# Attention rounds of 11, 10 and 11 key tiles in place of rounds of 8, and the output weights made in the last stage

## The chip, the cores and the metric

The kernel runs on one core of a Trainium2 chip. The metric is the device time of one execution in microseconds; lower is better. Every number below is from the hardware profiler's record of one execution, or from the times of unprofiled runs.

The core has a matmul engine (TensorE, PE in the profile, with its weight loads shown as PEld), three other compute engines (VectorE or DVE, ScalarE or ACT, GpSimd or POOL) and SyncE (SP), which here only starts transfers. Each works through its own queue in order. An instruction that needs another engine's result waits for a semaphore, and everything queued behind it on its engine waits with it. Matmul results go to PSUM, eight banks of 128 x 512 float32, and must be read from there by DVE or ACT before the bank can be used again.

## The reference

S = 2048 tokens, D = 448 features, H = 16 heads of 28 features, F = 1792 hidden features. What matters here:

```
g = sigmoid((x * gate_w).sum(-1, keepdims=True))
q, k, v = (x @ wqkv) per head
a = softmax(q k^T * 28 ** -0.5) @ v, heads joined, @ wo
gate = x @ W_gate;  up = x @ W_up
b = (relu(gate) * up) @ W_down
out = g * a + (1 - g) * b
```

## The kernel before, in words

Large matmuls run on float32r numbers; products of weights and tokens are made of a high and a low part of each, in 11 terms (`TERMS`, `NT = 11`) per output tile. The program has three stages.

**Projections.** q, k and v are made for all heads, and q and k go to memory. Between them stand the first matmuls of the softmax maxima.

**Attention rounds.** This is the long stage, and the change is in it. For a head, scores are computed as 16 key tiles of 128 keys by 2048 queries, and each key tile as 4 matmuls of 512 queries (`scores`, L202), which ACT turns into exp values in a buffer of 128 x 2048 (`P` slot, L204). The row maxima that the exp needs come from a separate pass over the transposed scores (`smax`, L175): 64 matmuls a head, each read by DVE with a maximum over 512 columns (L176). When a head's 64 are done, the maxima are transposed on PE (`smax_end`, L183) and sent by ACT, POOL and a transfer into two extra rows of `Q`, so that the scores come out with the maximum already subtracted. The maxima run 24 key tiles ahead of the scores. In the same stage PE makes the gated layer: a unit is 128 hidden features for 512 tokens, and has two halves, gate and up, of 11 matmuls each (`gu_mm`, L497). ACT applies relu to the gate half (`relu`), DVE multiplies it with the up half and POOL sends the product to memory (`spill_h`).

The order of these matmuls on PE is written out by hand as strings, one letter a matmul: `s` a score matmul, `m` a maximum matmul, `x` a matmul of the gated layer. `h` stands for the last of the 11 matmuls of two halves together: it needs only 64 of the array's 128 rows, so the two run side by side, each on its own rows (a pair). A round is one string followed by `pv`, which multiplies the exp values of all the round's key tiles with V (L531), four 32-column matmuls side by side, and adds into `OS` on DVE. There are `NP = 8` P slots, so a round has 8 key tiles and a head two rounds: 32 rounds, one with `FIRST`, 28 with `LONG` or `WIDE` (30 or 40 `x`, three or four halves), three with `LATE`.

Each kind of matmul has its own PSUM banks: `ps_s` gives the scores banks 0 and 1 in turn, `ps_m` gives the maxima banks 3 and 2 in turn, `ps_f` gives the halves 4, 5, 6, 7. At the start of a round `later` lends the scores and maxima a bank of a half that has not begun. In the `LATE` rounds, which have no maxima left, `ps_p` turns the scores through banks 0 to 3.

At a round's end ACT and POOL split the weights of the next units into high and low parts (`split_f`) and SP fetches the raw weights after them (`fetch_f`, two buffers). `small_things` starts the loads of K and Q two heads ahead, and handles the softmax denominators of the head before: the sums leave `OS` by a transfer (`ls`, L540), DVE takes reciprocals (`row_sums`, L545), they go out (`l_d`) and come back spread over the partitions (`spread`, `rb`, L552), and `normalise` multiplies `OS` with them and sends it out (`o_d`).

In the `LATE` rounds the output weights come back from memory (`load_wo`) and are split into high and low parts (`split_wo`); their tile `WO` is held in the attention stage's memory.

**Last stage.** The remaining units, the down projection (`down`, L751) and the output projection (`wout`, L706) alternate on PE by a list `todo`. SP fetches what they need (`fetch_d`: `wdr` and `hr`), and ACT, DVE and POOL split it (`split_d`).

Of the kernel before, what the change touches and what calls it, by code (L numbers as in the profile page):

```python
# [8 lines left out]
F32 = mybir.dt.float32  # L9
# [9 lines left out]
P = 128  # L19
S = 2048  # L20
# [21 lines left out]

FIRST = "ssssssssssssssssmmmmssulxxxsxxxsxmmsxsxxmmxsxsmmxxsxsmmxsxsxmmsxsxxmmssx"

LONG = "smsmxsmmsxxsmxsmxsmxsmxsmxsmxsmxsmxsmxsmxsmxsmxsmxsmxsmxsmxsmxsmxsmxsmxsmxsmxsmxsmxsmxsmxsmxsm"
WIDE = "smsmxsmmsxxsmxsmxsmxxsmxsmxsmxxsmxsmxsmxxsmxsmxsmxxsmxsmxxsmxsmxsmxxsmxsmxsmxxsmxsmxsmxxsmxsmxsmxxsmxsmxhh"
# [22 lines left out]
def gated_mix_kernel(ctx, tc, x, wq, wo, wgu, wd, out):  # L71
# [19 lines left out]
    def ps_s():  # L91
        return banks[turn("s", (0, 1))]
# [16 lines left out]
    def ps_f():  # L109
        return banks[turn("f", (4, 5, 6, 7))]  # L110

    def later(n):

        return banks[4 + (count["f"] + 1 + n) % 4]

    def act_high(dst, src):
        nc.scalar.activation(dst, src, AF.Copy)  # L117
# [76 lines left out]

    PT = {}

    def scores(i, j, ps=None):
        h, kt = divmod(i, NK)
        if j == 0:
            PT[i] = p_slot(i % NP, f"P_{i}")  # L200
        ps = ps or (ps_s() if i < NI - 3 * NK // 2 else ps_p())
        nc.tensor.matmul(ps, K[h % 3][:GD + 2, kt * P:(kt + 1) * P], Q[h][:GD + 2, j * TB:(j + 1) * TB],  # L202
                         start=True, stop=True)
        nc.scalar.activation(PT[i][:, j], ps, AF.Exp, scale=SCALE)  # L204
# [18 lines left out]
    with tc.tile_pool(name="qkv", bufs=1) as pa:  # L223
# [146 lines left out]
        x1 = load_x(1)  # L370


        warm = const.tile([P, TB], BF16, name="warm")
        nc.vector.memset(warm, 0.0)
        ps = ps_x()
        for n in range(WARM):
# [49 lines left out]
        for n, (f, *a) in enumerate(mixed):  # L426
            if n == 0:
                split_w(*w5)
            if n == 6:
                load_k(1)  # L430
                load_q(1)
            if n == 8:
                split_w(*w3)
            if n == 13:

                nc.gpsimd.memset(f32(K[2])[96:128], -1.0)
            if n == len(mixed) - 6:
# [8 lines left out]
            news = [(scores, *divmod(k, NB)) for k, back in enumerate(EARLY) if back == len(mixed) - n]  # L446
# [18 lines left out]
    att = stk.enter_context(tc.tile_pool(name="att", bufs=1))  # L465

    done = sum(n for _, n in ROUNDS) // 2
    SECOND = set(range(ROUNDS[0][1] + 1, 2 * done, 2))

    def lane(k):  # L470
        return slice(64 * k, 64 * k + 64)
# [19 lines left out]
    def gu_mm(ps, i, s, n):  # L491

        a, b = (BY_CHUNK if i else HIGH_FIRST)[n]
        rows = slice(0, P)
        if n == NT - 1 and 2 * i + s in SECOND | {k - 1 for k in SECOND}:
            rows = lane(int(2 * i + s in SECOND))
        nc.tensor.matmul(ps, WS[i][rows, s, a], xf(i // NF, b)[rows], start=(n == 0), stop=(n == NT - 1))  # L497
# [23 lines left out]

    OS, LS = {}, {}

    def pv(i0, ni):

        h = i0 // NK
        po = ps_w() if i0 == 0 else ps_m() if i0 < NI - 3 * NK // 2 else ps_p()
        for i in range(i0, i0 + ni):
            p = PT.pop(i)
            for j in range(NB):  # L530
                nc.tensor.matmul(po[32 * j:32 * j + 32], V[:, h // 4 % 2, i % NK, h % 4], p[:, j], start=(i == i0),  # L531
                                 stop=(i == i0 + ni - 1))
        if i0 % NK == 0:
            OS[h] = fe.tile([P, TB], F32, name=f"os_{h}", tag="os", bufs=2)
            nc.vector.tensor_copy(OS[h], po)  # L535
        else:
            nc.vector.tensor_tensor(OS[h], po, OS[h], op=OP.add)  # L537
        if (i0 + ni) % NK == 0:
            LS[h] = fe.tile([P, 16], F32, name=f"ls_{h}", tag="ls", bufs=2)
            nc.gpsimd.dma_start(LS[h], OS[h][DH::32].rearrange("j (p c) -> j p c", c=16))  # L540
# [26 lines left out]
    def load_wo():  # L567
        r = f32(q_slot("wor"))
        nc.sync.dma_start(r[:, 0:3, :D], wo_d[0:3 * P].rearrange("(c p) n -> p c n", p=P))
        for a in (0, 64):  # L570
            nc.sync.dma_start(r[a:a + 64, 3, :D], wo_d[3 * P:])
        return r[:, :, :D]

    def split_wo(r):
        dve_high(WO[:, 0:3], r[:, 0:3])
        pool_low(WO[:, 3:6], r[:, 0:3], WO[:, 0:3])
        dve_high(WO[:, 6], r[:, 3])
        pool_low(WO[64:, 6], r[64:, 3], WO[64:, 6])

    nxt = parts = i0 = 0  # L580

    def small_things(u):

        h, q = divmod(u, 4)

        if q == 0 and h and h + 2 < H:
            load_k(h + 2)
            load_q(h + 2)
        if u in (16, 32):
            g = u // 16 + 1  # L590
            nc.sync.dma_start(V[:, g % 2], v_d[g])
        if u == 2:
            pack_wo()
        if h and q == 2:
            row_sums(h - 1)
            spread(h - 1)

    split_f(0, act_high, pool_low, (0,))
    fetch_f(1)
    wor, units = None, []  # L600
    for r, (order, nu) in enumerate(ROUNDS):
        ni = order.count("s") // NB
        late = order == LATE
        todo = list(range(nxt, nxt + nu))
        nxt += nu
        small_things(i0 // 4)
        rest = []
        if m % (4 * NK) == 0 and i0 <= NI - LEAD:
            rest = smax_end(m // (4 * NK) - 1, later(2))
            rest.pop(0)()  # L610
            while late and rest:
                rest.pop(0)()
        if late and wor is None:
            wor = load_wo()

        passes = [(*divmod(k, 2), n) for k in todo for n in range(NT - (r > 0))]
        ns = 0
        for n, o in enumerate(order):
            if o == "s":
                i, j = i0 + ns // NB, ns % NB  # L620
                if ns == 4 * NB:
                    small_things(i0 // 4 + 1)
                if len(EARLY) <= i * NB + j:

                    scores(i, j, later(1) if r and ns == 2 and not late else None)
                ns += 1
                if rest and ns == 3:
                    rest.pop(0)()
            elif o == "m":

                smax(m, ps_w() if r == 0 else later(1) if order[:n].count("m") == 1 else ps_m())
                m += 1
            elif o == "x":
                i, half, k = passes.pop(0)
                if k == 0:
# [5 lines left out]
            elif o == "l":  # L641
                sends.pop()()
            elif o == "u":
                split_f(0, act_high, pool_low, (1,))
                load_k(2)
                load_q(2)
                fetch_f(2)
                parts = 2
            elif o == "h":
                ends, units = units[:2], units[2:]  # L650
                for i, half, ps in ends:
                    gu_mm(ps, i, half, NT - 1)
                for i, half, ps in ends:
                    spill_h(i, ps) if half else relu(i, ps, late)
        assert not passes, (r, passes)

        ready = nxt + (ROUNDS[r + 1][1] if r + 1 < len(ROUNDS) else 2)
        ready += ready % 2
# [6 lines left out]
        if i0 == NK // 2:  # L665
            gates()
        if i0 > NK and i0 % NK:
            normalise(i0 // NK - 1)
        pv(i0, ni)
        i0 += ni  # L670
        if late and i0 == NI - NK // 2:
            split_wo(wor)
    assert i0 == NI and m == 4 * NK * H and not units, (i0, m)
    stk.close()


    pf = ctx.enter_context(tc.tile_pool(name="ffn", bufs=1))
    ON, OR, GA, DR, HH, ACC = {}, {}, {}, {}, {}, {}

    def fetch_o(tb):  # L680
        OR[tb] = r = pf.tile([P, 4, TB], F32, name=f"or_{tb}", tag="or", bufs=1)
# [110 lines left out]
    for tb, load, split, at in ((0, 2, (3, 4), (5, 6, 7, 8)), (1, 5, (7, 9), (10, 11, 14, 14)), (2, 21, (23, 25), (28,) * 4),  # L792
# [57 lines left out]
```

## Time and profile before

| | before |
|---|---|
| unprofiled, median of 3 runs | 1287.82 us (1287.38 to 1288.04) |
| profiled execution | 1288.35 us, span 1286.6 us, granted TensorE clock 0.999 |
| PE busy / PEld busy | 1280.6 us / 920.3 us |
| DVE busy / ACT busy / POOL busy | 899.2 / 782.3 / 373.1 us |
| instructions | 18247, of them 6687 matmuls |

The span is the time from the first to the last instruction of the profiled execution. In a row of the timeline stand the start (us), the length (us), the engine, the line, the operation, output<-input, the shape and the number of instructions merged; in brackets the idle time before it and what ended it. In a row of the windows stand the stretch, its length, and the busy time of each engine. Matmuls are pipelined: a matmul of 512 columns is recorded as some 0.4 us long while the next one starts after a shorter step, so the steps between starts tell what PE spends.

### The profile page before, as it was taken

To read this page: it belongs to the slowest core of one execution; us is meant where nothing else is said; L and a number is where in the kernel's file an instruction comes from. 1 tells how busy PE (TensorE), PEld (TensorE's weight loads), DVE (VectorE), ACT (ScalarE), POOL (GpSimd) and SP (SyncE) were. 2 spreads that over 40 slices of the span, in tenths; PEclk is the share of its full clock that TensorE was granted. 3 is DMA by queue.
4 is the path that set the end of the run, shared out by engine and by line. 5 is a ranking of instruction groups with operands and counts; after the bars stand their busy time and mean duration, and the time that the engine had idled before them with its cause. 6 is when DMAs were issued, how large, how long until landed. Compare 5 with 4: busy or idle time off the path is not lost.

```text
span 1286.6 us, 18247 instructions
## 1 busy us (share of the span) xinstructions
PE 1280.6 (100%) x6687; PEld 920.3 (72%) x6687; DVE 899.2 (70%) x1351; ACT 782.3 (61%) x1433; POOL 373.1 (29%) x567
## 2 busy tenths in 40 slices
PE   9999999999999999999999999999999999999998
PEld 6888766666666666666666666666666666899997
DVE  6598787788788788888877788888888213653342
ACT  5212666777777777777776677777777776222121
POOL 3222232324223322222332423223131354651020
PEclk9999999999999999999999999999999999999999
DMA  8936434141425224141534142332431324634432
GB/s 315 294 148 245 130 101 94 58 121 58 115 79 175 85 64 114 35 114 34 147 110 121 52 112 77 89 89 67 89 125 33 96 86 149 210 131 142 139 107 78
DMA packets 53569, 148.89 MB, mean 116 GB/s; under 512 B 10024, under 2 KB 17128, under 8 KB 48872
## 3 DMA queue, kind: packets, MB, share of 16 engines
q1 hardware_dynamic: 36120, 98.34, 27.0%
q0 software_dynamic: 16928, 48.93, 10.8%
q8 instruction: 52, 0.85, 0.3%
q10 hardware_dynamic: 432, 0.46, 0.1%
q14 instruction: 37, 0.30, 0.1%
HBM read 102.06 MB, written 46.02 MB: 115 GB/s over the span
## 4 chain that ended last, share of the span: by engine, by line
PE 97%; DMA 2%; SPq 0%; ACT 0%; POOL 0%; issue 0%; DVE 0%; ACTq 0%
PE b L497 22%; PE b L202 19%; PE b L175 18%; PE b L531 17%; PE b L751 11%; PE b L332 5%; PE b L350 3%; PE b L706 3%; DMA qk_d<-pair 1%; DMA wgr<-wgu 0%; DMA wr<-wq 0%; PE b L183 0%; SPq L283 0%; ACT wg L117 0%; POOL wg L126 0%; SPq L166 0%
## 5 line engine op out<-in xcount | busy, mean ns | idle before, releaser
L176 DVE TENSOR_REDUCE mx<-b 128x1 f32<-128x512 f32 x1024 | 695.4, 689 | 29.2 <-PE b L175 20.3
L204 ACT ACTIVATE P<-b 128x512 f32<-128x512 f32 x768 | 449.6, 598 | 157.3 <-PE b L202 99.6
L497 PE MATMUL b<-X,wg 128*128 128x512 f32 (+1 forms) x1232 | 434.7, 401 | 0.0
L202 PE MATMUL b<-Q,K 114*128 114x512 f32 x1024 | 408.1, 399 | 0.2
L175 PE MATMUL b<-K,Q 112*128 112x512 f32 x1024 | 399.8, 396 | 0.0
L497 PEld LDWEIGHTS b<-X,wg 128*128 128x128 f32 (+1 forms) x1232 | 222.9, 190 | 56.8 <-issue 12.0
L202 PEld LDWEIGHTS b<-Q,K 114*128 114x128 f32 x1024 | 194.5, 190 | 57.7 <-issue 13.4
L175 PEld LDWEIGHTS b<-K,Q 112*128 112x128 f32 x1024 | 192.5, 188 | 50.7 <-DVE mx L176 4.1
L519 POOL DMA_DIRECT2D h_d<-h x56 | 31.4, 560 | 589.7 <-DVE h L513 475.1
L531 PE MATMUL b<-P,V 128*32 128x512 f32 x1536 | 177.3, 594 | 0.0
L204 ACT ACTIVATE V<-b 128x512 f32<-128x512 f32 x256 | 150.8, 599 | 26.9 <-PE b L202 4.3
L126 POOL TENSOR_TENSOR wg<-wgr,wg 128x384 fp32r<-128x384 f32 x204 | 146.4, 732 | 10.8 <-ACT wg L117 2.4
L751 PE MATMUL b<-WD,hh 128*128 128x448 f32 x672 | 140.9, 368 | 0.0
L751 PEld LDWEIGHTS b<-WD,hh 128*128 128x128 f32 x672 | 126.1, 188 | 12.8
L531 PEld LDWEIGHTS b<-P,V 128*32 128x32 f32 x1536 | 46.6, 110 | 106.0 <-issue 103.0
L117 ACT ACTIVATE hh<-hr 128x512 fp32r<-128x512 f32 x56 | 35.2, 631 | 124.6 <-PE b L751 122.5
L123 DVE TENSOR_TENSOR hh<-hr,hh 128x512 fp32r<-128x512 f32 x56 | 45.4, 810 | 67.1 <-ACT hh L117 67.1
L332 PE MATMUL b<-X,W 128*128 128x512 f32 x308 | 84.0, 397 | 0.6 <-DVE X L123 0.4
L535 DVE COPY os<-b 128x512 f32<-128x512 f32 x16 | 11.1, 692 | 87.8 <-PE b L531 87.8
L117 ACT ACTIVATE wg<-wgr 128x384 fp32r<-128x384 f32 x165 | 66.0, 482 | 9.0 <-DMA wgr<-wgu 6.3
L332 PEld LDWEIGHTS b<-X,W 128*128 128x128 f32 x308 | 57.8, 189 | 15.2 <-DVE X L123 2.0
L537 DVE TENSOR_TENSOR os<-b,os 128x512 f32<-128x512 f32 x16 | 11.1, 692 | 74.8 <-PE b L531 74.8
(69 smaller groups left out, 677.8 us busy)
## 6 DMA issues: line engine op xcount, KB each, us to landing
wgr<-wgu SPq DMA_DIRECT2D x55, 512.0 KB
K<-qk_d SPq DMA_DIRECT2D x64, 224.0 KB
Q<-qk_d SPq DMA_DIRECT2D x64, 224.0 KB
h_d<-h POOLq DMA_DIRECT2D x56, 256.0 KB, 2.6
hr<-h_d SPq DMA_DIRECT2D x56, 256.0 KB
qk_d<-st POOLq DMA_DIRECT2D x21, 512.0 KB, 3.7
x_d<-X POOLq DMA_DIRECT2D x6, 1024.0 KB, 5.0
X<-x_d SPq DMA_DIRECT2D x24, 256.0 KB
```

The lines of the kernel that those rows point to most:

```text
L117: nc.scalar.activation(dst, src, AF.Copy)
L123: nc.vector.tensor_tensor(dst, src, f32(high), op=OP.subtract)
L126: nc.gpsimd.tensor_tensor(dst, src, f32(high), op=OP.subtract)
L175: nc.tensor.matmul(ps, Q[h][:GD, u * P:(u + 1) * P], K[h % 3][:GD, c * TB:(c + 1) * TB], start=True, stop=True)
L176: nc.vector.tensor_reduce(MX[h][:, 4 * u + c:4 * u + c + 1], ps, axis=AX.X, op=OP.max)
L202: nc.tensor.matmul(ps, K[h % 3][:GD + 2, kt * P:(kt + 1) * P], Q[h][:GD + 2, j * TB:(j + 1) * TB], start=True, stop=True)
L204: nc.scalar.activation(PT[i][:, j], ps, AF.Exp, scale=SCALE)
L332: nc.tensor.matmul(ps, W[:, a, c * P:(c + 1) * P], xf(tb, b), start=(n == 0), stop=(n == NT - 1))
L350: nc.tensor.matmul(ps[:, :VC], xf(tb, b)[:, t * P:(t + 1) * P], W[:, a, 2 * D:], start=(n == 0), stop=(n == NT - 1))
L497: nc.tensor.matmul(ps, WS[i][rows, s, a], xf(i // NF, b)[rows], start=(n == 0), stop=(n == NT - 1))
L531: nc.tensor.matmul(po[32 * j:32 * j + 32], V[:, h // 4 % 2, i % NK, h % 4], p[:, j], start=(i == i0), stop=(i == i0 + ni - 1))
L751: nc.tensor.matmul(ACC[i // NF][t][:, :D], HH[i][:, a, t * P:(t + 1) * P], WD[:, f, b], start=(f == 0 and n == 0), stop=(f == NF - 1 and n ...
```

## The change

Rounds now have 11, 10 and 11 key tiles, so that three rounds make two heads, and the middle one finishes one head and begins the next. Three more P slots are made for it (`NP = 11`). There are 24 rounds: one with `FIRST`, seven times `TWO`, `THREE`, `ONE`, then `LATE` and `FINAL`. Every round but the last two has two units, that is four halves whose last matmuls run as two pairs at the round's end (`hh`); `LATE` and `FINAL` have three units each, the first of which is not paired. One unit more is left to the last stage.

Capital letters take the place of `later`: `S` is a score matmul in bank 6 and `M` a maximum matmul in bank 7, the banks of a round's third and fourth half (`ps_late`). `t` in `THREE` is the transposition of a head's maxima inside the round; other heads have it at the start of a round. `U` splits the weights of one more unit inside a round: in `FIRST` with ACT, in `LATE` and `FINAL` with DVE. The maxima run 21 key tiles ahead of the scores. In a round that spans two heads `pv` runs once for each. The pieces of `small_things` come by key tile (every fourth) and not at the start and the middle of a round, and `normalise` at the end of the round in which `row_sums` ran.

`WO` and its raw buffer move to the memory of the last stage: `load_wo` is the first transfer there, ahead of the first `fetch_d`, and `split_wo` stands ahead of the first `down`. The raw buffer shares its place with the one that `fetch_o` fills later.

```
-LONG = "smsmxsmmsxxsmxsmxsmxsmx...smxsm"
-WIDE = "smsmxsmmsxxsmxsmxsmxxsm...xsmxhh"
-LATE = "sxsxsxsxx" * 8 + "hh"
-TWO = [(LONG + "h", 3), (LONG + "hh", 3)]
-ROUNDS = [(FIRST, 2)] + (TWO + [(WIDE, 4)]) * 2 + TWO
-ROUNDS += ([(WIDE, 4)] + TWO * 4) * 2 + TWO + [(LATE, 4)] * 3
-NP = 8
+FIRST = ("ssssssssssssssssmmmmssulxxxxsxmxsxsxmSxsxsxmSxsxUsxmxsxsxmxsxsxmxsxsxmxsxsxmxsxsxmxsxsxmxsxsxmxsxsxm"
+         "xsxhh")
+ONE = ("smsMxSmxsmxsMxsmxsmxsmSMxsmxsmxsmxsmxsmxsmxsmxsmxsmxsmSMxsmxsmxsmxsmxsmxsmxsmxsmxsmxsmMsxmsxmsxMsxms"
+       "xmsxmsxmsxmsxmsxmsxmsxmsxmsxhh")
+TWO = ("msMsxmSxmsxMsxmsxmsxmsxmsxmsxmsxmsxmsxmsxmsxmsxmsxmsxmsxmsxmsxmsxmsxmsxmsxmsxmsxmsxmsxmsxmsxmsxms"
+       "xmsxmsxmsxmsxmsxmsxxhh")
+THREE = ("msMsxmSxmsxMsxmsxmsMxsmxsmxsmxsmxsmSxmsxmsxmsMxsmxsmxsmxsmxsmxsmxsmMsxtsxmsxMsxmsxmsxmsxmsxmsMxsm"
+         "xsmxsmxsmxsmxsmxsmxsmxsmxsmxshh")
+LATE = ("sxsxxsxsxxsxsxx...sxUsxxsxsxx...xxhh")
+FINAL = ("sxsxxsxsxxsxsxx...sxUsxxsxsxsxsx...sxsxxhh")
+ROUNDS = [(FIRST, 4)] + [(TWO, 4), (THREE, 4), (ONE, 4)] * 7 + [(LATE, 6), (FINAL, 6)]
+NP = 11
...
-    def later(n):
-        return banks[4 + (count["f"] + 1 + n) % 4]
+    def ps_late(kind):
+        return banks["SM".index(kind) + 6]
...
+            elif o == "t":
+                rest = smax_end(min(M), ps_m())
+                rest.pop(0)()
...
+            elif o == "U":
+                split_f(parts // 2, dve_high if late else act_high, pool_low)
+                parts += 2
+                fetch_f(parts // 2 + 1)
...
+        while summed:
+            normalise(summed.pop())
+        for a in {i0, max(i0, (i0 + ni) // NK * NK)}:
+            n = min(i0 + ni, (a // NK + 1) * NK) - a
+            if n > 0:
+                pv(a, n, ps_p if late else ps_m)
...
-    WO = fe.tile([P, 7, D], F32R, name="WO")
+    WO = pf.tile([P, 7, D], F32R, name="WO")
+    wor = pf.tile([P, 4, TB], F32, name="wor", tag="or", bufs=1)[:, :, :D]
...
+    before(0, (split_wo,))
+    load_wo()
     for i in range(4):
         fetch_d(i)
```

More of the change, by code (lines that the diff above doesn't have):

```diff
@@ L195, in gated_mix_kernel, with scores @@
     PT = {}
-    def scores(i, j, ps=None):
+    def scores(i, j, ps):
         h, kt = divmod(i, NK)
@@ L370, in gated_mix_kernel @@
         x1 = load_x(1)
-        warm = const.tile([P, TB], BF16, name="warm")
+        warm = pa.tile([P, TB], BF16, name="warm")
         nc.vector.memset(warm, 0.0)
@@ L445, in gated_mix_kernel @@
                 m += 1
-            news = [(scores, *divmod(k, NB)) for k, back in enumerate(EARLY) if back == len(mixed) - n]
+            news = [(scores, *divmod(k, NB), ps_s()) for k, back in enumerate(EARLY) if back == len(mixed) - n]
             for k, c in enumerate(news):
@@ L467, in gated_mix_kernel @@
     done = sum(n for _, n in ROUNDS) // 2
-    SECOND = set(range(ROUNDS[0][1] + 1, 2 * done, 2))
+    SECOND, nxt = set(), 0
+    for _, n in ROUNDS:
+        nxt += n
+        SECOND |= {nxt - 3, nxt - 1}
+    PAIRED = SECOND | {k - 1 for k in SECOND}
     def lane(k):
@@ L494, in gu_mm @@
         rows = slice(0, P)
-        if n == NT - 1 and 2 * i + s in SECOND | {k - 1 for k in SECOND}:
+        if n == NT - 1 and 2 * i + s in PAIRED:
             rows = lane(int(2 * i + s in SECOND))
@@ L522, in gated_mix_kernel, with pv @@
     OS, LS = {}, {}
-    def pv(i0, ni):
+    def pv(i0, ni, ps):
         h = i0 // NK
-        po = ps_w() if i0 == 0 else ps_m() if i0 < NI - 3 * NK // 2 else ps_p()
+        po = ps()
         for i in range(i0, i0 + ni):
@@ L596, in small_things @@
             spread(h - 1)
+            summed.append(h - 1)
+    summed = []
     split_f(0, act_high, pool_low, (0,))
     fetch_f(1)
-    wor, units = None, []
+    units = []
     for r, (order, nu) in enumerate(ROUNDS):
-        ni = order.count("s") // NB
-        late = order == LATE
+        ni = order.lower().count("s") // NB
+        late = order in (LATE, FINAL)
         todo = list(range(nxt, nxt + nu))
         nxt += nu
-        small_things(i0 // 4)
         rest = []
-        if m % (4 * NK) == 0 and i0 <= NI - LEAD:
-            rest = smax_end(m // (4 * NK) - 1, later(2))
+        if M:
+            rest = smax_end(min(M), ps_late("S"))
             rest.pop(0)()
@@ L612, in gated_mix_kernel @@
                 rest.pop(0)()
[L613 to L619, printed above, removed]
+        passes = [(*divmod(k, 2), n) for k in todo for n in range(NT - (k in PAIRED))]
+        ns = nm = 0
+        for o in order:
+            if o in "sS":
                 i, j = i0 + ns // NB, ns % NB
-                if ns == 4 * NB:
-                    small_things(i0 // 4 + 1)
+                if j == 0 and i % 4 == 0:
+                    small_things(i // 4)
                 if len(EARLY) <= i * NB + j:
-                    scores(i, j, later(1) if r and ns == 2 and not late else None)
+                    scores(i, j, ps_late(o) if o == "S" else ps_p() if late else ps_s())
                 ns += 1
-                if rest and ns == 3:
+                if rest and ns > 2:
                     rest.pop(0)()
-            elif o == "m":
-                smax(m, ps_w() if r == 0 else later(1) if order[:n].count("m") == 1 else ps_m())
+            elif o in "mM":
+                smax(m, ps_late(o) if o == "M" else ps_w() if r == 0 and nm < 4 else ps_m())
                 m += 1
+                nm += 1
+            elif o == "t":
+                rest = smax_end(min(M), ps_m())
+                rest.pop(0)()
             elif o == "x":
@@ L654, in gated_mix_kernel @@
                     spill_h(i, ps) if half else relu(i, ps, late)
-        assert not passes, (r, passes)
-        ready = nxt + (ROUNDS[r + 1][1] if r + 1 < len(ROUNDS) else 2)
-        ready += ready % 2
+        assert not passes and not units, (r, passes)
+        ready = nxt + (4 if r + 1 < len(ROUNDS) else 2)
         while parts < ready:
@@ L663, in gated_mix_kernel @@
                 fetch_f(parts // 2 + 1)
-        if i0 == NK // 2:
+        if r == 1:
             gates()
-        if i0 > NK and i0 % NK:
-            normalise(i0 // NK - 1)
-        pv(i0, ni)
+        while summed:
[4 more added lines that the diff above has]
+                pv(a, n, ps_p if late else ps_m)
         i0 += ni
-        if late and i0 == NI - NK // 2:
-            split_wo(wor)
-    assert i0 == NI and m == 4 * NK * H and not units, (i0, m)
+    assert i0 == NI and m == 4 * NK * H, (i0, m)
     stk.close()
@@ L678, in gated_mix_kernel, with load_wo, split_wo @@
     ON, OR, GA, DR, HH, ACC = {}, {}, {}, {}, {}, {}
+    WO = pf.tile([P, 7, D], F32R, name="WO")
+    wor = pf.tile([P, 4, TB], F32, name="wor", tag="or", bufs=1)[:, :, :D]
+    def load_wo():
+        nc.sync.dma_start(wor[:, 0:3], wo_d[0:3 * P].rearrange("(c p) n -> p c n", p=P))
+        for a in (0, 64):
+            nc.sync.dma_start(wor[a:a + 64, 3], wo_d[3 * P:])
+    def split_wo():
+        dve_high(WO[:, 0:3], wor[:, 0:3])
+        pool_low(WO[:, 3:6], wor[:, 0:3], WO[:, 0:3])
+        dve_high(WO[:, 6], wor[:, 3])
+        pool_low(WO[64:, 6], wor[64:, 3], WO[64:, 6])
     def fetch_o(tb):
```

21 lines of the change are left out of this document (6 added, 15 removed).

## The prediction

> **What bounds the kernel now.** I read the page's busy shares and its chain first, then the windows of single rounds, then the timeline of PE at a round's end.
>
> ```profile
> PE 1280.6 (100%) x6687; PEld 920.3 (72%) x6687; DVE 899.2 (70%) x1351; ACT 782.3 (61%) x1433; POOL 373.1 (29%) x567
> PE 97%; DMA 2%; SPq 0%; ACT 0%; POOL 0%; issue 0%; DVE 0%; ACTq 0%
> L176 DVE TENSOR_REDUCE mx<-b 128x1 f32<-128x512 f32 x1024 | 695.4, 689 | 29.2 <-PE b L175 20.3
> ```
>
> 97% of the chain is PE, so the time is the sum of PE's steps and of what makes PE late. DVE is the next busy engine; it reads 1024 maxima of 0.69 us. The windows of three rounds and of one `pv`:
>
> ```profile
> 618.77:641.39 22.62, 22.62 (x101) 17.93 (x97) 22.05 (x33) 19.00 (x32) 4.27 (x8) 1.00 0.69 183
> 641.39:648.39 7.00, 7.00 (x66) 1.97 (x65) 1.28 (x3) 1.76 (x5) 3.46 (x5) 1.00 0.21 54
> 648.39:671.22 22.83, 22.83 (x104) 17.88 (x100) 22.41 (x34) 19.55 (x35) 3.98 (x8) 1.00 0.26 83
> 678.22:703.38 25.16, 25.16 (x112) 19.94 (x108) 22.50 (x34) 19.15 (x33) 4.26 (x8) 1.00 0.46 123
> ```
>
> The third and fourth rows are rounds with 94 and 104 letters and two pairs each: ten letters cost 25.16 - 22.83 = 2.33 us, 0.233 a letter (0.2337 over all). The first row has 94 letters and one pair: a pair costs 22.83 - 22.62 = 0.21, say one letter. 22.83 - 94 x 0.2337 - 2 x 0.234 leaves 0.40 us that belongs to the round itself; 25.16 treated in the same way leaves 0.39, so it doesn't grow with the round. The timeline shows where it lies:
>
> ```profile
> 610.78 0.39 PE L175 MATMUL b<-K,Q 112*128 112x512 f32 x1
> 611.10 0.73 PE L497 MATMUL b<-X,wg 64*128 64x512 f32 x4
> 611.76 4.50 PE L531 MATMUL b<-P,V 128*32 128x512 f32 x40
> 618.77 0.50 PE L202 MATMUL b<-Q,K 114*128 114x512 f32 x1
> 619.11 0.40 PE L175 MATMUL b<-K,Q 112*128 112x512 f32 x1
> 619.34 0.40 PE L202 MATMUL b<-Q,K 114*128 114x512 f32 x1
> ```
>
> The step into the pairs is 0.32 in place of 0.23, two pairs take 0.66 in place of 0.47, and the second letter after `pv` comes 0.34 after the first. `pv` itself: 40 matmuls in 4.50 us are ten steps of four, 0.43 each; 16 of them are 6.88 of its 7.00 us, so 0.12 is once per `pv`. A round thus costs 0.40 + 0.12 = 0.52 us beyond its matmuls.
>
> **What the change does to the sum.** The sum is made against the profiled execution, 1288.35 us, which is 0.53 above the median of 1287.82.
>
> *Rounds, 32 to 24.* 8 x 0.52 = -4.2 us. The matmuls of `pv` stay; in seven rounds it runs as two groups back to back, which I put at +0.1 in all (a bank change within `pv` is in no row; between nothing and 7 x 0.12).
>
> *Pairs.* Before, all halves but the first two are paired, 50 pairs; now 24 rounds have two, 48. Four more letters and two pairs fewer: 4 x 0.234 - 2 x 0.234 = +0.5. The unit that moves to the last stage costs the same letters there. The transposition inside `THREE` costs what it costs at a round's start.
>
> *A bank that is still being read.* This is the term that decides. How long a bank is held:
>
> ```profile
> 69.98 0.40 PE L175 MATMUL b<-K,Q 112*128 112x512 f32 x1
> 70.41 0.69 DVE L176 TENSOR_REDUCE mx<-b 128x1 f32<-128x512 f32 x1 [0.23 <-PE b L175]
> ...
> 589.90 3.10 DVE L176 TENSOR_REDUCE mx<-b 128x1 f32<-128x512 f32 x5
> 590.47 0.62 PE L175 MATMUL b<-K,Q 112*128 112x512 f32 x2
> 590.59 0.19 PEld L175 LDWEIGHTS b<-K,Q 112*128 112x128 f32 x1 [0.16 <-DVE mx L176]
> 590.93 0.39 PE L202 MATMUL b<-Q,K 114*128 114x512 f32 x1
> ...
> 649.19 0.24 DVE L545 RECIPROCAL rs<-ls 128x16 f32<-128x16 f32 x1
> 649.35 3.10 DVE L176 TENSOR_REDUCE mx<-b 128x1 f32<-128x512 f32 x5
> ```
>
> The maximum begins 0.43 us after its matmul began and lasts 0.69; queued maxima follow each other at (3.10 - 0.69) / 4 = 0.60, and a reciprocal takes 0.16 of DVE's stream. And what PE does when a reader is late:
>
> ```profile
> 148.68 1.10 ACT L204 ACTIVATE P<-b 128x512 f32<-128x512 f32 x2
> 148.69 0.63 PE L175 MATMUL b<-K,Q 112*128 112x512 f32 x2
> 149.34 0.19 PEld L202 LDWEIGHTS b<-Q,K 114*128 114x128 f32 x1 [0.46 <-ACT P L204]
> 149.35 0.50 PE L202 MATMUL b<-Q,K 114*128 114x512 f32 x1
> 149.69 0.40 PE L497 MATMUL b<-X,wg 128*128 128x512 f32 x1
> ```
>
> The weight load holds the wait. The first exp ended at 149.28 (the two are 0.50 apart and last 0.60), the load began at 149.34, and the letter behind it came at 149.69. From the letter ahead (148.92, the second of its row) to 149.69 two steps took 0.77 in place of 0.47. So PE goes on as if the late letter had begun 0.17 us after its reader's end.
>
> Before, a bank of the maxima comes back after six letters, 6 x 0.234 = 1.40 us, and 0.43 + 0.69 + 0.17 = 1.29 fits. In the changed order bank 7 is lent to an `M` shortly before the fourth half begins in the same bank with its 31st `x`. In `THREE` the string there is `m s M x s m [x]`: the `x` is due four letters after `M`, 0.93 us. The `m` ahead of it holds DVE until -0.47 + 0.43 + 0.60 = 0.56; the maximum of `M` ends at 1.25, PE goes on at 1.42, 0.49 us late. Seven rounds: +3.4 us. Its lower end is DVE free for `M`, 1.29 - 0.93 = 0.36, +2.5. In `ONE` it is `m M s x m s x m s x M s x m s [x]`, and the `x` comes five letters after the last `M`. From the first `m` of this row: maxima begin at 0.43, 1.03, 1.63 and 2.23; then stands the reciprocal of the head before (its key tile begins two letters ahead of the last `M`), so that the last `M` begins at 2.99, ends at 3.68, and PE goes on at 3.85; the `x` is due at 15 letters, 3.51. Seven rounds at 0.34: +2.4; with DVE free only 1.29 - 1.17 = 0.12, +0.8. Nothing gives these losses back, since PE waits for nothing else that they would cover.
>
> The Trainium skill bears on this (PSUM — Partial Sum Buffer, section Engine vs sequencer instructions): weight loads overlap running matmuls, but matmuls start and complete in program order. By that rule the `s` and `m` behind the blocked `x` can't fill the gap, and the sum keeps the +5.8; the five rows above agree.
>
> *The first round.* Before, it and the next lost twice: 0.30 us at 149.35, and here:
>
> ```profile
> 145.11 0.36 SPq L220 DMA_DIRECT2D wgr<-wgu  x1
> ...
> 165.31 1.25 ACT L117 ACTIVATE wg<-wgr 128x384 fp32r<-128x384 f32 x3 [5.27 <-DMA wgr<-wgu]
> ...
> 166.24 0.40 PE L497 MATMUL b<-X,wg 128*128 128x512 f32 x1
> 166.76 0.50 PE L202 MATMUL b<-Q,K 114*128 114x512 f32 x1
> 167.10 0.63 PE L175 MATMUL b<-K,Q 112*128 112x512 f32 x2
> ```
>
> ACT waited until 165.31 for raw weights, its exps came late, and two steps took 0.86 in place of 0.47. ACT had come to these copies at 160.04. Now `FIRST` has 30 letters and two pairs more, so it comes to them 7.9 us later, when the weights are there, and this 0.39 goes; 0.7 is saved. But `U` puts three copies on ACT (1.25 as in the row above, 1.14 of ACT's stream) where two scores come every five letters: 1.17 us for 2 x 0.50 of ACT, so the backlog lasts and scores find banks 0 and 1 occupied. I take 0.9 there and 0.5 at the `s` near 149 (one bank sooner than before): 1.4, net +0.7, between -0.7 and +1.0. The raw weights of `U`, issued at 145.11, have landed by then if they take no longer than those behind the wait.
>
> *The last stage.* 896 KB of output weights go ahead of the first `wdr` and `hr`, while the DMA engines are full:
>
> ```profile
> wor<-wo_d SPq DMA_DIRECT2D x1, 672.0 KB
> wor<-wo_d SPq DMA_DIRECT2D x2, 112.0 KB
> ...
> 1086.75:1091.75 5.00, 5.00 (x23) 4.00 (x22) 3.80 (x6) 3.40 (x7) 2.25 (x3) 1.00 1.05 401
> ...
> 1087.32 0.63 ACT L117 ACTIVATE hh<-hr 128x512 fp32r<-128x512 f32 x1 [2.09 <-DMA wdr<-wd]
> ...
> 1089.20 0.68 DVE L123 TENSOR_TENSOR hh<-hr,hh 128x512 fp32r<-128x512 f32 x1
> ```
>
> At 401 GB/s they take 2.3 us. The first `hh` would be whole at 1089.88 + 2.3 = 1092.2 on the old clock, against a first `down` after two units of 22 letters, 1081.75 + 10.3 = 1092.1, if all of the delay came through. The rate in the 5 us before is lower, and part of the wait before was for transfers that don't stand behind the new ones; I take 0, between 0 and +2.4. DVE's and POOL's copies for `WO` follow the first two `split_d`, and PE needs them only at the fifth `down`: hidden.
>
> *Other moves, costed at nothing.* The exps of `LATE` are 2 x 0.50 against five letters of 1.17. K and Q are loaded a round ahead as before. At a round's end ACT and POOL split four halves while `pv` runs 9.6 us (11 key tiles), against POOL's 7.2 us of work (below).
>
> Sum: -4.2 + 0.1 + 0.5 + 3.4 + 2.4 + 0.7 = +2.9. From 1288.35 that is 1291.3, and 1290.7 against the median.
>
> **The rivals.**
>
> *Not slower: the blocked `x` costs PE little.* Without the losses at bank 7, 1290.7 - 5.8 = 1284.9. It decides between gain and loss at (5.8 - 2.9) / 14 = 0.21 us a place. For it speaks that the weight load at 590.59 came 0.16 late and the steps to 590.70 and 590.93 stayed at 0.23; against it that two that came later still cost 0.30 and 0.39. The Trainium skill (TensorE: Matmul & The Clock Gate, its opening table, engine queue depth) gives PE's queue a partial reorder window; were `s` and `m` let through, this time would come out; no row here shows a matmul overtaking another.
>
> *Half of them:* with both places at their lower ends, 2.5 + 0.8, the time is 1288.2, no change.
>
> *Slower: DVE waits for the sums of a head.*
>
> ```profile
> 613.25 1.15 POOL L519 DMA_DIRECT2D h_d<-h  x2 [17.57 <-DVE h L513]
> 614.42 6.05 POOL L126 TENSOR_TENSOR wg<-wgr,wg 128x384 fp32r<-128x384 f32 x8
> 622.46 0.73 POOL L540 DMA_DIRECT2D ls<-os  x1
> ...
> DMA to landing us min/median/max: 3.3/8.2/11.1
> ```
>
> For every second head `ls` is now issued after POOL's splits at the end of `TWO`, some 9.4 us behind the pairs (620.47 - 611.10), and the reciprocal stands at the fourth key tile of `THREE`: 0.7 of pairs, two `pv` of 8.7, 35 letters of 8.2 and the start, 17.8 us behind them. That leaves 8.4 us. If it lands after 11.1, DVE stands 2.7 us with the maxima queued behind it, and PE after some 0.2 of slack: 7 x 2.5 = +17, 1308. It begins to cost at 8.6. For it: the median is 8.2. Against it: four `o_d` and the loads of K and Q crowded `ls` before, and neither starts there now. The Trainium skill (DMA: Bandwidth & Descriptors, section Issuing engines are not separate DMA queues) says that transfers from all engines interleave on the same 16 DMA engines; that is why the crowd matters.
>
> *The saving isn't there:* if a round's 0.52 grew with its length, 4.2 would go, 1294.9; the equal 0.40 and 0.39 speak against it.
>
> **How the numbers follow.** Within 0.2% (2.6 us) a measurement of this kernel can hardly tell a change. Forecast, slower by about 2.9: 0.52, itself between 1288.5 and 1293.5, so some of it lies within 0.2%. Half of the losses: 0.20. None: 0.16. DVE waits in some part: 0.07. No saving: 0.05. Of the forecast 0.32 is beyond 1290.4 and 0.20 within. Slower 0.32 + 0.07 + 0.05, within 0.2% 0.20 + 0.18, faster 0.16 + 0.02. The range leaves out the late `ls` and the far ends: 1284.3 to 1294.0.
>
> **What would show it.** PE's busy stays near 100% of the span, but its weight loads show idle time before L506 ended by DVE's maxima, about 7 x 0.5 and 7 x 0.3. A round of 128 letters and two pairs takes 128 x 0.2337 + 0.47 + 0.40 = 30.8 us and a `pv` of 11 key tiles 22 x 0.43 + 0.12 = 9.6; `THREE` shows 31.3 and `ONE` 31.1. No DVE idle time ended by `ls` in the rounds, none of PE ahead of the first `down`. The prediction is wrong if these losses are absent, or if another wait takes the chain from PE.

## The result and the profile after

The changed kernel takes 1291.81 us in the median of nine runs (1290.60 to 1292.30) against 1288.04 for the kernel before beside it (nine runs, 1287.38 to 1288.68). The ratio is 1.0027, with a 95% interval of 1.0017 to 1.0038: slower by a quarter of a per cent. The forecast was 1290.7. The profiled execution took 1290.85 us with a span of 1289.1, 2.5 us over the one of before. The medians say 3.8. Of the other 1.3, 0.3 is that the profiled execution before lies above its kernel's median (1288.35 against 1288.04), and 1.0 that the changed kernel's lies below its own (1290.85 against 1291.81). That 1.0 can't be seen in this profile; two of the experiments below find it.

The first view is the page: busy shares, the shares of the chain, and three groups with their idle time.

```profile
PE 1281.0 (99%) x6687; PEld 923.2 (72%) x6687; DVE 893.6 (69%) x1361; ACT 778.4 (60%) x1427; POOL 369.6 (29%) x563
PE 96%; DVE 3%; ACT 1%; DMA 0%; issue 0%; SPq 0%; DVEq 0%
L506 PE MATMUL b<-X,wg 128*128 128x512 f32 (+1 forms) x1232 | 438.8, 401 | 1.5 <-DVE mx L182 1.5
L207 PE MATMUL b<-Q,K 114*128 114x512 f32 x1024 | 406.0, 397 | 1.0 <-ACT V L209 0.7
```

PE has as many matmuls as before and the same busy time within 0.4 us, but the chain now leaves PE for DVE's maxima and for an exp of ACT. Those are the two places to look at. The windows of one `TWO`, its `pv`, one `THREE`, its `pv` and one `ONE` (columns as before: stretch, length, busy time and count of each engine):

```profile
176.65:205.56 28.91, 28.91 (x129) 22.99 (x125) 27.84 (x41) 24.35 (x43) 1.41 (x3) 1.00 0.34 83
205.56:214.28 8.72, 8.72 (x82) 2.50 (x80) 3.66 (x6) 3.32 (x9) 6.83 (x10) 1.00 0.34 118
214.28:245.60 31.32, 31.10 (x137) 24.34 (x133) 30.02 (x47) 26.21 (x47) 4.68 (x9) 1.00 0.12 28
245.60:255.18 9.58, 9.58 (x90) 2.76 (x88) 1.89 (x3) 3.27 (x9) 7.67 (x12) 1.00 0.35 112
255.18:286.17 30.99, 30.98 (x136) 24.41 (x132) 30.25 (x47) 26.14 (x45) 4.43 (x9) 1.00 0.39 93
```

`TWO` has 120 letters and two pairs: 28.91 - 122 x 0.2337 = 0.40, the body's share of a round as before. `THREE` and `ONE` have 128 letters: 31.32 and 30.99 leave 0.94 and 0.61 by the same sum (0.08 of the 0.94 is the step after the transposition in the middle of `THREE`; in `ONE` slightly quicker letters hide some of the loss, so the steps below show 0.27 and not 0.21). The timeline shows where, first in `THREE`, then in `ONE`:

```profile
235.94 2.58 DVE L182 TENSOR_REDUCE mx<-b 128x1 f32<-128x512 f32 x4
236.67 0.40 PE L181 MATMUL b<-K,Q 112*128 112x512 f32 x1
237.37 0.39 PE L181 MATMUL b<-K,Q 112*128 112x512 f32 x1
237.98 0.19 PEld L506 LDWEIGHTS b<-X,wg 128*128 128x128 f32 x1 [0.65 <-DVE mx L182]
237.98 0.50 PE L506 MATMUL b<-X,wg 128*128 128x512 f32 x1 [0.22 <-DVE mx L182]
238.31 0.39 PE L207 MATMUL b<-Q,K 114*128 114x512 f32 x1
...
277.43 0.39 PE L181 MATMUL b<-K,Q 112*128 112x512 f32 x1
277.93 0.24 DVE L554 RECIPROCAL rs<-ls 128x16 f32<-128x16 f32 x1
278.09 1.22 DVE L182 TENSOR_REDUCE mx<-b 128x1 f32<-128x512 f32 x2
278.37 0.40 PE L207 MATMUL b<-Q,K 114*128 114x512 f32 x1
278.77 0.19 PEld L506 LDWEIGHTS b<-X,wg 128*128 128x128 f32 x1 [0.45 <-DVE mx L182]
278.77 0.50 PE L506 MATMUL b<-X,wg 128*128 128x512 f32 x1
279.11 0.39 PE L181 MATMUL b<-K,Q 112*128 112x512 f32 x1
```

In `THREE` the matmul at 236.67 is the `M` in bank 7. The fourth half's first `x` follows the letter at 237.37 after 0.61, the next one after 0.33: 0.47 more than two steps of 0.234. In `ONE` the same two steps are 0.40 and 0.34, 0.27 more. All seven rounds of each show it, within 0.02. The first round:

```profile
149.34 0.19 PEld L207 LDWEIGHTS b<-Q,K 114*128 114x128 f32 x1 [0.69 <-ACT P L209]
...
153.24 1.24 ACT L123 ACTIVATE wg<-wgr 128x384 fp32r<-128x384 f32 x3
...
155.02 0.50 PE L207 MATMUL b<-Q,K 114*128 114x512 f32 x1 [0.73 <-ACT V L209]
```

The two scores come 0.41 and 0.90 late, and each costs another 0.10 at the next letter: 1.51 us. And the sums of a head in `THREE` (the view of one tile, in the window of one round):

```profile
L549 POOL DMA_DIRECT2D ls<-os x1: 725/725/725, 215.4 to 215.4; - x1
L554 DVE RECIPROCAL rs<-ls x1: 243/243/243, 223.3 to 223.3; 128x16 f32<-128x16 f32 x1
DMA to landing us min/median/max: 2.9/2.9/2.9
```

They land 2.9 us after their issue (2.9 to 4.0 over the seven rounds) and are read 7.9 us after it (6.7 and 6.2 in two rounds): DVE doesn't wait. The sums of the other heads, issued at the start of `ONE`, where the DMA share is 0.39 and not 0.12 as in `THREE`, take 7.1 to 8.7 us in six of seven rounds, and are read 21.6 us after their issue.

Two lengths serve for all runs below: attention, from the last projection's matmul to the first `x` of the last stage, and the last stage, from there to its last matmul, both read off the matmuls' starts in the profiled execution. The kernel before was run beside each batch of runs, and its median moved by 0.8 us between batches with nothing changed (1287.23 to 1288.05); so a few tenths between medians of different batches say nothing.

| kernel | attention, us | last stage, us | PE's wait in the last stage | median, us |
|---|---|---|---|---|
| before | 937.07 | 200.43 | 0 | 1287.23 to 1288.05 |
| changed | 933.96 | 206.06 | 0 | 1291.81 |
| THREE alone | 930.66 | 206.22 | 0.2 | 1287.41 |
| ONE alone | 932.18 | 206.49 | 0.4 | 1290.01 |
| U on DVE | 932.91 | 207.84 | 1.8 | 1290.78 |
| these three | 927.60 | 206.06 | 0 | 1284.62 |

### The profile page after: what moved, and what is told of

Its sections match the earlier page's. It is cut to its first block, busy times and chain, and to the rows that moved or that the text cites. A ratio compares the mean times of both kernels' runs of the same rounds, so it can differ in the third digit from the quotient of the medians.

```text
span 1289.1 us, 18216 instructions
## 1 busy us (share of the span) xinstructions
PE 1281.0 (99%) x6687; PEld 923.2 (72%) x6687; DVE 893.6 (69%) x1361; ACT 778.4 (60%) x1427; POOL 369.6 (29%) x563
## 4 chain that ended last, share of the span: by engine, by line
PE 96%; DVE 3%; ACT 1%; DMA 0%; issue 0%; SPq 0%; DVEq 0%
PE b L506 21%; PE b L181 18%; PE b L207 18%; PE b L540 17%; PE b L764 11%; PE b L337 6%; DVE mx L182 3%; PE b L719 3%; PE b L355 3%; DMA wr<-wq 0%; PE b L189 0%; ACT wg L123 0%; ACT V L209 0%; ACT P L209 0%; SPq L288 0%
## 5 line engine op out<-in xcount | busy, mean ns | idle before, releaser
L182 DVE TENSOR_REDUCE mx<-b 128x1 f32<-128x512 f32 x1024 | 685.6, 688 | 30.7 <-PE b L181 23.5
L209 ACT ACTIVATE P<-b 128x512 f32<-128x512 f32 x840 | 493.7, 598 | 157.5 <-PE b L207 90.1
L540 PE MATMUL b<-P,V 128*32 128x512 f32 x1680 | 188.2, 593 | 0.0
L132 POOL TENSOR_TENSOR wg<-wgr,wg 128x384 fp32r<-128x384 f32 x200 | 143.0, 731 | 11.3 <-ACT wg L123 3.1
L540 PEld LDWEIGHTS b<-P,V 128*32 128x32 f32 x1680 | 52.7, 110 | 121.3 <-issue 116.9
L209 ACT ACTIVATE V<-b 128x512 f32<-128x512 f32 x184 | 108.0, 598 | 43.4 <-PE b L207 28.7
L555 POOL DMA_DIRECT2D l_d<-rs x16 | 8.9, 559 | 205.1 <-DVE rs L554 205.1
L123 ACT ACTIVATE wg<-wgr 128x384 fp32r<-128x384 f32 x159 | 63.1, 486 | 5.5 <-DMA wgr<-wgu 2.7
```

Of the source, the lines that this page charges most:

```text
L132: nc.gpsimd.tensor_tensor(dst, src, f32(high), op=OP.subtract)
L182: nc.vector.tensor_reduce(MX[h][:, 4 * u + c:4 * u + c + 1], ps, axis=AX.X, op=OP.max)
```

## The losses at bank 7 and at U, taken away one by one

*The M of THREE.* It moves nine letters ahead, so that the fourth half's first `x` comes 13 letters after it:

```
-THREE = ("...mMsxtsxmsxMsxmsxmsxmsxmsxmsMxsm"
+THREE = ("...mMsxtsxmsxMsxmsxmsMxsmxsmxsmxsm"
```

> THREE alone: its last M stands 13 letters ahead of the fourth half instead of 4; everything else as in the changed kernel. Theory (bank 7 is still being read by the maximum of that M): the two steps of 0.61 and 0.335 us at the fourth half's first x become 0.234 each, 0.475 us in each of seven rounds, -3.3 us: 1288.5 against the changed kernel's 1291.8, and no step takes the lost time over elsewhere. Rival (THREE simply has more maxima than DVE takes, so the wait moves to another bank): 0 to -1 us, and steps above 0.28 us appear at other letters of THREE.

Attention is 930.66, 3.30 less than in the changed kernel, as the first theory has it; the steps at the fourth half are 0.234, and no other letter of `THREE` comes late. The page agrees:

```profile
PE 99%; ACT 0%; DMA 0%; DVE 0%; issue 0%; DVEq 0%
L506 PE MATMUL b<-X,wg 128*128 128x512 f32 (+1 forms) x1232 | 438.2, 400 | 0.0
```

DVE is out of the chain. So the place of one letter cost it, not the number of maxima. The median fell further, by 4.4. 0.35 of that the kernel before shows as well between the two batches (1288.04 and 1287.69); the rest belongs to a wait in the last stage that is taken up below.

*The M's of ONE.*

```
-ONE = ("...xsmxsmxsmxsmxsmxsmMsxmsxmsxMsxms"
+ONE = ("...xsmMsxmsxmsxMsxmsxmsxmsxmsxmsxms"
```

> ONE alone: its M's of the third half stand 29 and 20 letters ahead of the fourth half instead of 14 and 5. Theory (the queue of maxima and the reciprocal ahead of the last M): the steps of 0.40 and 0.335 at the fourth half's first x become 0.234, 0.27 in each of seven rounds, -1.9 us: 1289.9. Rival (the reciprocal alone makes DVE late by 0.16 and whatever comes next pays it): -0.8 us and a step above 0.28 at an m or s behind the reciprocal.

Attention is 1.78 shorter and the median 1.8. No step above 0.28 stands behind the reciprocal, so the rival falls: with two banks in turn DVE's being late by 0.16 costs nothing where no bank is due.

*U's copies on DVE.*

```
-split_f(parts // 2, dve_high if late else act_high, pool_low)
+split_f(parts // 2, dve_high, pool_low)
```

> First round: the copies of U go to DVE instead of ACT. Theory (the three copies on ACT make the exps late and a score finds its bank occupied): the steps of 1.13 and 0.335 around 155.0 become 0.234, -1.0 us: 1290.8. Rival (DVE's maxima come late instead): 0, a wait of a matmul for mx in the first round. The score near 149.3 keeps its 0.65 by both.

Attention is 1.05 shorter, the median 1.0. The score at 155 is in time; the one at 149.1 keeps its step of 0.64.

*The three together.*

> The three edits together. If the three losses are independent they add: -3.3 -1.9 -1.0 = -6.2 us, 1285.6, which is 2.4 us (0.19%) under the kernel before. If they share a cause (DVE's queue), less: about 1287 to 1288.

Attention is 927.60, 6.36 less: -3.30, -1.78 and -1.05 make -6.13, so the three add up within 0.23. The median is 1284.62, 0.9979 of the kernel before (0.9970 to 0.9988).

## The same fault put where there was none

*An M two letters ahead of the fourth half, in TWO.*

```
-TWO = ("...xmsxmsxms"   (then the fourth half's first x)
+TWO = ("...xmsxmsxMs"
```

> TWO, which loses nothing so far, gets the fault on purpose: the maximum two letters ahead of its fourth half's first x uses bank 7 in place of bank 2 or 3. Theory (the reader's end decides; from the matmul, 0.43 to the maximum, 0.69 of it, 0.17 to PE, against two letters, 0.47): 0.82 in each of seven rounds, split as about 0.72 at the x and 0.10 at the next letter, +5.7 us: 1297.5 against the changed kernel's 1291.8. Rival (s and m behind the blocked x go ahead of it in PE's queue): under 0.2 a round, below +1.5 us, and letters recorded between the late weight load's start and its x.

Attention is 939.68, 5.72 longer, against 5.7 expected. The timeline of one place (198.24 is the `M`, 199.41 the `x`):

```profile
198.24 0.40 PE L181 MATMUL b<-K,Q 112*128 112x512 f32 x1
198.47 0.39 PE L207 MATMUL b<-Q,K 114*128 114x512 f32 x1
199.41 0.19 PEld L506 LDWEIGHTS b<-X,wg 128*128 128x128 f32 x1 [0.98 <-DVE mx L182]
199.41 0.50 PE L506 MATMUL b<-X,wg 128*128 128x512 f32 x1 [0.56 <-DVE mx L182]
199.75 0.39 PE L181 MATMUL b<-K,Q 112*128 112x512 f32 x1
```

Between 198.47 and 199.41 PE starts no matmul, though the `m` and `s` behind the `x` have their banks free. The rival of a queue that lets them through falls, and the loss can be counted off in letters: 0.82 at two letters' distance, 0.47 at four, nothing at 13.

## What a late sum would have cost

*The reciprocal two key tiles earlier in THREE.*

```
-        if h and q == 2:
+        if h and q == 2 and (u % 8 != 6 or u == 62):
...
+                if j == 0 and i % 32 == 22 and i < 240:
+                    sums(i // NK - 1)
```

> In THREE the reciprocal of a head's sums and what follows it stand two key tiles (24 letters, 5.6 us) earlier. In the changed kernel the sums land 2.9 to 4.0 us after their issue, and the reciprocal starts 8.0 us after it (6.7 and 6.2 in two rounds). Theory (DVE stands until the sums are there, all maxima wait behind it, and PE runs out of banks): the reciprocal would come 2.4 us after the issue (0.6 to 1.1 in the two), DVE stands 0.5 to 2.5 us a round, PE loses that less 0.2: 5 x 0.5 + 2 x 2.2, about +7 us, 1299. Rival (two banks of the maxima and DVE's own slack cover it): within 1 us of 1291.8.

The median is 1299.48 (1299.31 to 1301.63), attention 942.24, 8.3 longer. Of this kernel, one line of the waits (in all, times, longest), the timeline of the worst round, and its windows of 1 us with PE alone (length, busy time, count, granted clock):

```profile
DVE rs L554 <- DMA ls<-os: 7.4, 7, 3.1
```

```profile
937.98 0.39 PE L207 MATMUL b<-Q,K 114*128 114x512 f32 x1
939.92 0.25 DVE L554 RECIPROCAL rs<-ls 128x16 f32<-128x16 f32 x1 [3.12 <-DMA ls<-os]
940.77 0.80 PE L181 MATMUL b<-K,Q 112*128 112x512 f32 x1 [2.41 <-DVE mx L182]
941.37 0.63 PE L506 MATMUL b<-X,wg 128*128 128x512 f32 x1
941.79 0.63 PE L207 MATMUL b<-Q,K 114*128 114x512 f32 x1
```

```profile
939.00:940.00 1.00, 0.00 (x0) 1.00 0.10 35
941.00:942.00 1.00, 1.00 (x3) 0.50 0.04 8
```

DVE's waits of 0.2 to 0.5 in five rounds cost PE 0.17 to 0.35, those of 2.7 and 3.1 cost 2.6 and 4.2 (the second with some 3 us of half the granted clock behind it). So the rival of the prediction had its mechanism and price right; it stayed away since the sums land in 2.9 to 4.0 us, not in 8.2. In the changed kernel itself the margin between landing and reading is 4.7 us or more in five rounds (7.9 - 3.2), but only 2.8 and 2.2 in the two whose reading comes early (6.7 - 3.9 and 6.2 - 4.0). The prediction had counted 8.4 us from issue to reading in all of them.

## The wait that the profiled execution did not have

The changed kernel's median lies 1.0 above its profiled execution. The profile of the run with `U` on DVE caught what can make such a difference: its last stage is 1.8 longer. Its DVE and POOL rows, and PE's:

```profile
1092.02 4.75 DVE L126 CAST WD<-wdr 128x448 fp32r<-128x448 f32 x1
1098.26 2.47 DVE L129 TENSOR_TENSOR wg<-wgr,wg 128x384 fp32r<-128x384 f32 x4
...
1091.38 2.01 POOL L561 DMA_DIRECT2D rb<-l_d  x4
1093.41 4.38 POOL L132 TENSOR_TENSOR WO<-wor,WO 128x1344 fp32r<-128x1344 f32 x2
...
1097.87 0.39 PE L506 MATMUL b<-X,wg 128*128 128x512 f32 x1
1099.79 0.97 PE L506 MATMUL b<-X,wg 128*128 128x512 f32 x3 [1.53 <-DVE wg L129]
```

A copy that takes 0.37 elsewhere takes 4.75, until 1096.77. POOL makes the low parts of the output weights from 1093.41 on, in two instructions of 3.11 and 1.19 (merged in the row), and the copy ends 0.26 after the first of them. DVE's low parts of gate and up weights then come late, and PE stands. The changed kernel has the same in another place (the first of its four low parts takes 4.10), and the kernel before in none: there POOL made these parts in a `LATE` round, while DVE had hardly more than a reciprocal to do. The changed kernel and the one before:

```profile
1093.81 6.90 DVE L129 TENSOR_TENSOR wg<-wgr,wg 128x384 fp32r<-128x384 f32 x4
1094.38 4.55 POOL L132 TENSOR_TENSOR WO<-wor,WO 128x1344 fp32r<-128x1344 f32 x2
```

```profile
1059.54 4.48 POOL L126 TENSOR_TENSOR WO<-wor,WO 128x1344 fp32r<-128x1344 f32 x2
1059.75 0.24 DVE L545 RECIPROCAL rs<-ls 128x16 f32<-128x16 f32 x1
```

The Trainium skill (SBUF — State Buffer, section SBUF: two separate sides) says that DVE and GpSimd share one pair of ports as a lock: a DVE instruction that reads two tensors in SBUF, or copies in a two-port mode, blocks fully while an instruction of GpSimd that reads SBUF holds it, and the one that starts first gets it. The end of the copy agrees, right behind POOL's instruction. Its start doesn't: it is recorded 1.39 us ahead of POOL's, while POOL still issues the transfers of `rb` (1091.38 to 1093.39). What holds DVE in that time is open.

*The low parts on DVE.*

```
-        pool_low(WO[:, 3:6], wor[:, 0:3], WO[:, 0:3])
+        low(WO[:, 3:6], wor[:, 0:3], WO[:, 0:3])
```

(and the same for the fourth chunk)

> The low parts of the output weights are made by DVE in place of POOL. In the last stage of four profiled runs one DVE instruction that reads two tensors or copies in SBUF took 4.75 to 4.85 us instead of 0.4 to 0.7 while POOL made these parts, and PE waited 0 to 1.9 us for low parts of gate and up weights from DVE, differently in each execution. Theory (DVE stands while POOL holds what they share, and what PE loses depends on which instruction is caught): no long DVE instruction, no PE wait in the last stage, times all in the lower group, 1290.6 to 1291.1, median -1.0. Rival (the wait comes from the late landing of the gate and up weights behind the output weights on SP's queue): the spread of 1290.6 to 1292.3 stays.

Eleven runs lie between 1290.30 and 1290.90, median 1290.58, 1.2 less (the kernel before took 1288.05 beside them, 1288.04 beside the changed one). DVE needs 1.56 and 0.62 for what took POOL 4.5, and the four low parts behind them are short again:

```profile
1092.18 1.56 DVE L129 TENSOR_TENSOR WO<-wor,WO 128x1344 fp32r<-128x1344 f32 x1
1094.08 0.62 DVE L129 TENSOR_TENSOR WO<-wor,WO 64x448 fp32r<-64x448 f32 x1
1095.64 2.51 DVE L129 TENSOR_TENSOR wg<-wgr,wg 128x384 fp32r<-128x384 f32 x4
```

With POOL's part gone, the spread of 1.7 us is 0.6. That settles it against the rival of a late landing, since the weights still stand behind the output weights on SP's queue. All nine profiles with POOL's part in the last stage have one DVE instruction of 4.1 to 4.85 us there, not the same one; five show a wait of PE: 0.2, 0.4, 1.4, 1.8 and 1.8 us.

## A rhythm of PE that no edit explains

A matmul with the output weights took 0.2045 us a step before and 0.2067 after, 0.4 us in all. Their address had changed, so it was tried by 32 bytes ahead of the last stage's tiles:

```
+    pf.tile([P, 8], F32, name="gap_wo")
     WO = pf.tile([P, 7, D], F32R, name="WO")
```

> 32 bytes are put ahead of the output weights and all tiles behind them in the last stage. Before the change the output weights stood at an address 32 past a multiple of 64 bytes and a matmul with them took 0.2045 us a step; now they stand at a multiple of 64 and it takes 0.2067. Theory (the address of the moving operand): the 176 output matmuls go back to 0.2045, -0.4 us, and the 672 down matmuls, whose weights shift too, go from 0.2066 to 0.2045, -1.4 us: 1290.0. Rival (something else, such as the order of the banks): both steps stay at 0.2067, no change.

Both steps went to 0.2027, lower than either kernel had, and the median to 1287.61. To use it, all that paid was put together (the three edits, the low parts on DVE, the 32 bytes, and the letter `u`'s copies on DVE):

> The edits that paid, together: the M's of THREE and ONE moved (-6.2 with the next), U's copies on DVE, the low parts of the output weights on DVE, the 32 bytes ahead of the last stage's tiles, and also the copies of the first round's second half (letter u) on DVE. If they are independent: 1284.6 with the first three, 848 steps of 0.2027 in place of 0.2067 in the last stage, -3.3, and the score at 149.3 in time, -0.5: 1280.7, which is 0.994 of the kernel before. If the first round's score waits for something other than ACT's copies, 1281.2.

1280.47 us (1280.33 to 1280.64), 0.9949 of the kernel before (0.9936 to 0.9961). Attention is 927.16, 0.44 under the three edits, and the score near 149 is in time, which the copies of `u` had held up. Then the 32 bytes were put at the head of the first pool, in this kernel and in the one before:

> The same, but with the 32 bytes at the head of the pool that lives through the whole kernel, so that the operands of all matmuls stand 32 past a multiple of 64. Theory A (the saved 4 ns is the same for every matmul): 3,020 letters of the rounds and 308 projections also lose 4 ns, -13 us on top: about 1267. Theory B (it is only so for rows of 448 numbers, and 512 aren't touched): the same as the run before it, 1280.7.

> The kernel before with the same 32 bytes at the head of the pool that lives through the whole kernel, and nothing else. If the step depends on the address alone, its 672 down matmuls go from 0.2065 to 0.2027 and its 176 output matmuls from 0.2045 to 0.2027, -2.9 us: 1285.1; with theory A of the run before it, -16 us. If the gain needs the changed kernel's layout: 1288.0.

The first gave 1284.73, both theories wrong: its output and down matmuls have the very addresses of the run ahead, yet take 0.2067. The second gave 1285.48 (0.9984), with steps that begin at 0.2067 in the last stage and end at 0.2027. Windows of 20 us, PE alone, of the quick and then of the slow kernel:

```profile
1160.00:1180.00 20.00, 20.00 (x101) 1.00 0.51 155
```

```profile
1160.00:1180.00 20.00, 20.00 (x99) 1.00 0.55 159
```

Two matmuls more in 20 us, both at a granted clock of 1.00. The last run took 64 bytes:

> The changed kernel with 64 bytes in place of 32 ahead of the last stage's tiles, so that its operands stand at a multiple of 64 again. If the position within 64 bytes sets the step, the down and output matmuls take 0.2067 as without any shift: 1291.8 (1290.6 to 1292.3). If any shift can put the stream of matmuls into the quicker rhythm, 0.2027: 1287.6.

Its ten times lie between 1287.01 and 1291.37, median 1289.08 (POOL's part is still in this kernel, so some of the spread is that), and its profile shows 0.2044 at first and 0.2027 from 40 us into the stage. That execution (1287.25) fits the second case expected; the median lies between the two. The two kernels that took 1280.47 and 1284.73 have the same addresses and different steps, so the address of the operands doesn't set the step. A stream of matmuls of 448 columns can run at a steady 0.2067, or in a pattern of steps from 0.199 to 0.207 with a mean of 0.2027 (0.2045 and 0.2022 occur as means too), and one kernel can change from one to the other; what picks it stays open. For this reason only 0.2% of the gain (the run with slow steps, 1284.73, 0.9971 to 0.9989) is put down to the edits, and the 4.3 us between it and 1280.47 to the rhythm (some 3.2) and to letters that took 1.1 less in attention.

## Why the prediction was right, and where not

*Rounds, pairs and pv.* Right: the body's 0.40 stays, a `pv` of 11 key tiles takes 9.58 (9.6 forecast), and 20 steps of four in two groups take 8.72, so the second group costs nothing in place of 0.1. The two late rounds have 0.1 less than the others each, -0.2, which the sum lacked.

*Bank 7.* Right in place and mechanism. `THREE` 0.475 a round against 0.49, +3.3. `ONE` was over-sized: 0.27 against 0.34, +1.9; the two maxima behind the reciprocal took 1.22 together, where 0.69 and 0.60 are 1.29; the first of them, the one of `M`, was 0.06 shorter, and the bank came back that much sooner. The rule on program order that stood beside it held also at the doubled fault in `TWO`.

*The first round.* 1.51 lost against 1.4; before, 0.69 was lost; +0.8 against +0.7. Moving the copies of `U` alone, and those of `u` among the edits of the quickest kernel, confirmed which ACT work it was.

*The last stage.* This step failed: "DVE's and POOL's copies for `WO` follow the first two `split_d`, and PE needs them only at the fifth `down`: hidden." PE indeed needs the output weights late, and the transfers ahead of `wdr` and `hr` cost nothing at the first `down`. But POOL's work on them held up DVE, whose low parts of gate and up weights PE needs 21 to 22 us into the stage: nothing in the profiled execution of the changed kernel, 0.2 to 1.8 in five others, 1.2 in the median. The queue of each engine was looked at, not what two engines share.

*The sum.* -4.2 - 0.2 + 0.5 + 3.3 + 1.9 + 0.8, and 0.4 of rhythm, are +2.5, as the profiled executions show (+2.9 forecast). The medians' +3.8 has 1.3 more: 0.3 from the profiled execution before, and some 1.0 to 1.2 from DVE and POOL. The sum also holds a term that nobody forecast: the rounds' plain steps have a mean of 0.2333 in the changed kernel and of 0.2337 before, and over 2880 of them that is some 1.0 us in its favour, hidden in the -4.2 - 0.2 since letters were priced at 0.2337. Kernels of nearly the same program have either mean (0.2333 at 1280.47, 0.2337 at 1284.73), so it need not be owed to the change. The forecast of +2.9 was near by errors that partly made up for each other, and to that extent by luck.

## What to carry to other kernels

When a schedule lends a bank, count the letters from the loan's last reader to the owner's first write, with the reader's queue ahead of it: here 1.29 us and more against four or five letters of 0.234 cost 5.2 us in seven rounds of each kind, more than the 4.2 that eight saved rounds had brought. Work taken off one engine's queue and put beside another's must be checked for what both share, and times that scatter more than their neighbours' are a reason to profile again. Where two variants differ by a few tenths of a per cent, compare the step of the plain matmul stream first, since it can move the whole by as much.

## What the runs showed of the hardware

A matmul held by a bank's late reader costs more than the wait: the step to it and another 0.10 at the next letter, in every place alike.

With no matmul begun for 2.8 us (2.41 idle), the granted clock fell to 0.50 for 3.4 us and steps became 0.427; after 2.33 us from one matmul's start to the next, in another round of the same kernel, it stayed at 1.00. The Trainium skill (TensorE: Matmul & The Clock Gate, section What's actually happening) has the clock fall after an idle window of about 3.4 us; here less was enough.

One DVE instruction stands until a POOL instruction of 3.11 us has ended, 4.75 in place of 0.37, and which one is caught differs between profiles whose program is the same in this place.

448-column matmuls step at 0.2067 or, on the mean, at 0.2027 us under the same granted clock and with the same addresses, unexplained.
